# Turning the next unit's AT, G and K at other places of VectorE's order in a fused RWKV-7 and mixture kernel

## The chip, the core and the metric

The kernel runs on one core of a Trainium2 chip. The core has five engines with a queue of instructions each, and each runs its queue in order: TensorE (PE) multiplies matrices, VectorE (DVE) and GpSimd (POOL) work element by element, ScalarE (ACT) copies and activates, SyncE (SP) here only issues transfers. They wait for each other by semaphores. The metric is the time of one execution on the device, in microseconds; lower is better. Before the change the median of three runs is 1080.93 us (1078.75 to 1084.01).

## The reference

Two blocks follow each other. The first is a recurrence over 768 steps for 4 x 8 heads of width 40:

```python
y[:, :, t] = np.einsum('bhd,bhde->bhe', rt, state)
Sa = np.einsum('bhde,bhe->bhd', state, at)
state_decay = state * wt[:, :, None, :] - np.einsum('bhd,bhe->bhde', Sa, bt)
state = state_decay + np.einsum('bhd,bhe->bhde', vt, kt)
```

Its output, 3072 tokens of width 320, goes into four experts with 1024 hidden values each, whose outputs are added by normalized weights:

```python
for e in range(E):
    h = np.maximum(x @ w1[e], 0.0)
    out += p[:, e:e + 1] * (h @ w2[e])
```

All of it is fp32.

## The kernel before, in words

**Units.** The 768 steps are cut into 12 chunks of 64, and the 4 batches into 2 pairs. A chunk of one pair is a unit, `u` = 0 to 23. Inside a unit the recurrence is written as products of matrices: the decays are multiplied up along time (G), K and N (from b) are divided by them, A (AT) is multiplied by them, and a triangular system is solved for each head. The mixture for a chunk begins when both of its units are done, and its products are woven between those of the later units, so TensorE always has dense products beside the small ones.

**From unit 8 on** (`BY_CHANNEL`) the inputs of the next units come as raw tiles with heads and time side by side, and VectorE turns them: `turn_raw` (L324), a stream transpose. In one turn of the loop over `u`, work for several units is mixed, in the program's names:

- *G of unit u+3*: two turns out of rawW (L520), a scan (L566) that multiplies up along time, and the reciprocal `gp` (L582). `G0` is a memset of a column of it (L529).
- *AT*: one turn out of rawA, and the product with G (`AG`, L626). VT and RT are turned likewise.
- *N and K*: two turns each, out of rawB and rawK, then one product with `gp` (L640 and L645).
- *M, Z*: `blocks` (L722) are copied from F, the result of the products pfe; M is a transpose of them (L730) with its diagonal cleared (`M0`, L736); Z1 (L742) and Z2 (L746) take the first step of the substitution on VectorE. GpSimd then runs 48 short steps on Z (L760, L777), one behind the other, some 23 us. VectorE turns the result into Qc (L793) and QTc (L794), which the products pY, pQ and psat need. `merge` holds these.
- *RH* (L844): the sum behind the products prn. *Y, state* (L913 to L925): what is read from the products pdy. *ET, SX, VC*: masked copies (L499).

**The mixture on VectorE.** For an expert, the products of the hidden values with w2 are done by a scheme with seven products in place of eight. `add_h` (L1104) makes the five A sums of the hidden values: `a1`, `a7`, `a5`, `a2`, `a6`, named `sum_a0`, `sum_a1`, ... over the whole kernel, ten in each unit, so two groups of five. `down_1` multiplies p431, whose third term has `a1`; `down_2` multiplies p75 and p26, which use the other four. Their results are added to `osb` (L991, L993: "adds"). `down_1` of an expert follows on TensorE soon after its A sums were made, `down_2` much later.

**What sets the order.** A scheduler orders each engine's instructions by its own estimates and by what waits for what. On top, the kernel holds a list of stated orders for VectorE: pairs (one, then) without a semaphore, which only say which of two instructions comes first. `pin` and `keep` hold an instruction in program order instead. SP's queue is in program order: `later` is a list of transfers that are begun a few at a time between the pieces of the mixture (`mix` calls `begin_later`), or all at once with `begin_later(len(later))`. `load_piece` (L404) loads 640 KB of w1 in three transfers once TensorE has released the buffer.

The raw tiles and `gp` have one buffer each, `G` has three and `AT` two.

Of the kernel before, what the change touches and what calls it, by code (L numbers as in the profile page):

```python
# [33 lines left out]
def kernel(  # L34
# [46 lines left out]
    NJ = H // 2  # L81
    NF = F // P
    NU = NC * B // 2
# [6 lines left out]
    def noted(ins, name, n=None, i=None):  # L90
        if n is None:
            n = sum(k.startswith(name) for k in made)
        key = f"{name}{n}" if i is None else f"{name}{n}.{i}"
        made[key] = ins
        if key in names:
            stated_order.append(ins)
        return ins

    def keep(ins):

        if not any(ins is x for x in stated_order):
            tc.keep_in_program_order(ins)
# [109 lines left out]
    BY_CHANNEL = 8  # L212
# [32 lines left out]
    EARLY = 5  # L245
# [39 lines left out]
    def load_raw(q, names):  # L285


        moves = []
        for x in names:
            q.n["raw" + x] = t = raw[x]()  # L290
            heads = srcs[x].rearrange("b h t e -> (b h) t e")[q.b[0] * H:(q.b[1] + 1) * H, q.c * L:(q.c + 1) * L, :]
            heads = heads.rearrange("n (x two) e -> x n (two e)", two=2)
            for r in range(2):
                if x in "RV":

                    sets = ((slice(0, 8, 2), slice(r, 16, 4)), (slice(1, 8, 2), slice(3 - r, 16, 4)))
                else:
                    sets = ((slice(0, 8), slice(r, 16, 2)),)
                for n, hs in sets:
                    for y, w_ in enumerate((D + Q, 2 * D - Q)):  # L300
                        o = slice(64 * r + Q * y, 64 * r + Q * y + Q)
                        moves.append(lambda eng, out=t[o, n, 0:w_], in_=heads[:, hs, Q * y:Q * y + w_]: eng.dma_start(out=out, in_=in_))
        return moves
# [18 lines left out]
    def turn_raw(out, t):  # L322

        return nc.vector.transpose(  # L324
            out=out.rearrange("p n (x two) -> p n two x", two=2),
            in_=t.rearrange("p n (two e) -> p n two e", two=2)[:, :, :, 0:Q],
        )
# [173 lines left out]
    def within(q):  # L501

        n = q.n

        def pin(ins, also=False):
            if q.u <= PADDED or also:
                keep(ins)
# [3 lines left out]
        G = sb.tile([P, 2 * NJ, L + 1], FP32, name="G", tag="G", bufs=3)  # L511
        flat = G[:].rearrange("p c t -> p (c t)")
        if by_channel:
            q.G = Gv = G[:, :, 0:L]
            ahead = G[:, :, 1:L + 1].rearrange("p (j i) t -> p i j t", i=2)
        else:
            q.G = Gv = flat[:, 0:2 * NJ * L].rearrange("p (c t) -> p c t", t=L)
            ahead = flat[:, 1:2 * NJ * L + 1].rearrange("p (j i t) -> p i j t", i=2, t=L)
        for i in range(2):
            pin(noted(turn_raw(ahead[:, i], n["rawW"][:, NJ * i:NJ * i + NJ, :]), "G", q.u, i), EARLY + 2 < q.u < BY_CHANNEL + 3)  # L520
        if by_channel:
            q.gl = G[:, :, L:L + 1]
        else:
# [647 lines left out]
    todo, last, later, stores, here = [], [], [], [], [0]  # L1171

    def begin_later(n):
        for move in later[:n]:
            tc.keep_in_program_order(move(nc.sync))
        del later[:n]

    def mix(n):

        for piece in todo[:n]:  # L1180
            ready = stores[:]
            del stores[:]
            piece()
            for begin_store in ready:
                begin_store()
            begin_later(6 if here[0] % 4 == 0 and n > 1 else 3 if n > 1 else 6)
        del todo[:n]
# [5 lines left out]
    def run(gen, n=99):  # L1193
        if gen is None:
            return
        for _ in range(n):
            if next(gen, gen) is gen:
                break
# [3 lines left out]
    def begin_step(u):  # L1202
        q = units[u]
        if q.bp == 0:
            chunks_x[q.c] = sb.tile([P, 3, 2 * P], FP32, name="xT", tag="xT", bufs=2)
        q.xT = chunks_x[q.c][:, :, q.bp * P:(q.bp + 1) * P]
        return step(q, q.xT)
# [103 lines left out]
    for u in range(1, NU):  # L1311
        in_order[0] = True
        q = units[u]
        m = s_next = w = w_next = iter(())
        if u + 1 < NU:
            m, s_next = merge(units[u + 1]), begin_step(u + 1)
            w_next = ws[u + 1]
        if u + 2 < NU:
            w = ws[u + 2]

        def gap(n, pieces=None):
            here[0] = at = 4 * u + n
            run(sum_ops, sums_at.get(at, 0))
            mix((1 if at in sparse else 2) if pieces is None else pieces)

        early = u < EARLY
        if early:
            begin_later(len(later))
        ahead = u + 3 < NU and u >= EARLY
        if ahead and u < EARLY + 3:  # L1330
            go(load_raw(begin(u + 3), "W"))
        if early:
            lead()
        if u == 1:
            run(s, 1)
            run(w_next)
        else:
            run(w_next, 99 if early else 1)
            if u == EARLY:
                lead()  # L1340
            run(s, 1)
        gap(0)


        if early:
            run(s, 1)
        run(w, 1)
        if not early:
            run(w_next)
            run(s, 1)  # L1350
            if BY_CHANNEL <= u + 2 < NU:
                load_tokens(units[u + 2])
            run(s)

        if early:
            run(w, 1)
            gap(1, 2 if u + 1 == EARLY else None)
            run(s)
        if u == 1:
            mixture_of_unit(q)  # L1360
        elif q.bp:
            mixture_of_chunk(units[u - 1:u + 1], chunks_x[q.c])
        if not early:
            begin_later(len(later))
            run(w, 1)
            lead()
            todo[:2] = todo[1::-1]
            gap(1)
            run(m, 1)

        if u + 3 < NU:
            if u == 1:
                go_now(load_raw(begin(4), "WVRA"))
            else:
                go(load_raw(units[u + 3] if ahead else begin(u + 3), "A" if ahead else "WA"))
            load(units[u + 3], "V" if u + 3 >= BY_CHANNEL else "WBKV")
            if u > 1:
                later.extend(load_raw(units[u + 3], "VR"))
        run(w, 2)
        if BY_CHANNEL <= u + 2 < NU:  # L1380
            scale_tokens(units[u + 2])

        soon = u in (2, 3, 4)
        if soon:
            run(w, 1)
        if early:
            run(m, 1)
        else:
            run(m, 1)
            run(s_next, 1)  # L1390
            lead()
            run(m, 1)
            if u + 3 < NU:
                ws.append(within(units[u + 3]))
                run(ws[u + 3], 1)
        if soon:
            substitute(units[u + 2], nc.gpsimd)
        gap(2)

        if u == 1:  # L1400
            run(s_next, 1)
            run(m, 1)
        if not soon:
            run(w, 1)
        if not soon and u + 2 < NU:
            with sooner(not early):
                substitute(units[u + 2], nc.gpsimd)
        if not early:
            lead()
            run(s_next, 1)  # L1410
        if early:
            run(w, 1)
        if early:
            ws.append(within(units[u + 3]))
            run(ws[u + 3], 1)
            if u > 1:
                run(m, 1)
                run(s_next, 1)
            run(m)
            if u == 3:  # L1420
                begin_later(len(later))
            gap(3, 1)
            run(s_next, 1)
        else:
            begin_later(len(later))
            if BY_CHANNEL <= u + 3 < NU:
                if u + 3 == BY_CHANNEL:
                    pad_raw()
                later.extend(load_raw(units[u + 3], "BK"))
            gap(3)  # L1430
        if u >= EARLY + 2 and u + 4 < NU:
            later.extend(load_raw(begin(u + 4), "W"))
        s = s_next
# [5 lines left out]
    turned_ahead += [("QTc6", x) for x in ("VC7.0", "VC7.1", "sum_w15", "sum_w16")]  # L1439
    waits_of_scalar = [(f"SXc0.{n}", "RTc1.0") for n in range(4)]  # L1440
    ahead_of_merge = [(f"{x}{u}", f"Qc{u - 1}") for u in range(BY_CHANNEL, NU) for x in "KN"]
    ahead_of_merge += [(f"G{u}.{i}", f"Qc{u - 2}") for u in range(BY_CHANNEL + 3, NU) for i in range(2)]
    ahead_of_merge += [(f"VC{u}.{r}", f"1/gp{u + 1}") for u in range(BY_CHANNEL, NU - 1) for r in range(2)]
    ahead_of_merge += [(f"RH{u - 1}.{r}", f"1/gp{u + 1}") for u in range(BY_CHANNEL, NU - 1) for r in range(2)]
    ahead_of_merge += [(f"QTc{u - 1}", f"RH{u - 1}.{r}") for u in range(BY_CHANNEL, NU) for r in range(2)]
    ahead_of_merge += [(f"QTc{u - 1}", f"VC{u}.{r}") for u in range(BY_CHANNEL, NU) for r in range(2)]
    ahead_of_merge += [(f"1/gp{u + 2}", f"sum_a{10 * u - 45 + n}") for u in range(BY_CHANNEL, NU - 2) for n in range(5)]
    ahead_of_merge += [(f"M{u}", f"AT{u + 1}") for u in range(BY_CHANNEL, NU - 1)]
    in_second = [("Zr1.14", "out0"), ("out0", "Zm1.16")]
    for one, then in [*zip(names, names[1:]), *((f"out{n}", x) for n, x in moved), ("blocks0.3", "VCv1"), ("blocks0.3", "ETc0.0"), ("blocks1.3", "Zu1.0"), ("blocks1.3", "Zu1.3"), *turned_ahead, *in_second, *waits_of_scalar, *ahead_of_merge]:  # L1450
        tc.add_manual_dep(made[then].ins, made[one].ins.name, BEHIND, reason="stated order of VectorE")
# [30 lines left out]
```

## Time and profile before

| what | us |
|---|---|
| median of three runs | 1080.93 |
| the profiled execution | 1080.12 |
| its span on the core | 1078.4 |
| TensorE busy | 1052.9 |
| VectorE busy | 793.6 |
| GpSimd busy | 536.6 |
| ScalarE busy | 344.4 |

The span is what the engines record from first to last; the profiled execution's own time has 1.7 us more around it. A row of the timeline gives start, duration, engine, line of the code, operation, output and inputs with their shapes, and in brackets the idle time of the engine before it and what ended that. Rows of a group are merged with their number at the end (x4), and a duration is then that of all together. The duration of a row on VectorE overlaps the next by some 0.1 us, so the distance from row to row is shorter than the durations. In the waits a line names who waited for whom, the us in total, how often, and the longest.

### The profile page before, as it was taken

How to read it: one execution, taken by the hardware profiler on the slowest of the kernel's cores; microseconds unless marked ns; L12 is line 12 of the kernel's file. 1: busy time of each engine (PE TensorE's matmuls, PEld its weight loads, DVE VectorE, ACT ScalarE, POOL GpSimd, SP SyncE). 2: the span in 40 equal slices, each digit the busy share in tenths (PEclk: the TensorE clock that was granted, in tenths of full speed). 3: DMA queues.
4: the chain of work that ended last, by engine and by line, in shares of the span. 5: the costliest groups of instructions: out<-in, count | busy, mean ns of one | idle time of the engine just before them, and what ended most of it. 6: DMA issues, size and time to landing. Idle time of an engine off the chain costs nothing.

```text
span 1078.4 us, 38527 instructions
## 1 busy us (share of the span) xinstructions
PE 1052.9 (98%) x16022; PEld 945.3 (88%) x16022; DVE 793.6 (74%) x1565; ACT 344.4 (32%) x942; POOL 536.6 (50%) x1322
## 2 busy tenths in 40 slices
PE   8999999999999999999999999999999999999998
PEld 7888878888899889898998898898988999998887
DVE  7787679898778877777877878768777786634343
ACT  3433444423333323324233333242333333221110
POOL 6117677756375474563663744745636547520000
PEclk9999999999999999999999999999999999999999
DMA  6776644344443443543553563454444443121220
GB/s 115 189 206 140 143 101 117 81 101 107 109 102 96 112 111 71 138 104 78 117 124 67 106 143 58 108 125 90 98 121 95 98 108 91 55 72 51 75 86 13
DMA packets 275350, 111.05 MB, mean 103 GB/s; under 512 B 229816, under 2 KB 254952, under 8 KB 275176
## 3 DMA queue, kind: packets, MB, share of 16 engines
q1 hardware_dynamic: 271192, 107.75, 43.6%
q8 instruction: 126, 2.06, 0.8%
q10 hardware_dynamic: 3984, 0.84, 0.4%
q14 instruction: 48, 0.39, 0.1%
HBM read 100.65 MB, written 3.93 MB: 97 GB/s over the span
## 4 chain that ended last, share of the span: by engine, by line
PE 65%; POOL 14%; DVE 8%; issue 5%; DMA 4%; SPq 2%; ACT 2%; DVEq 0%; ACTq 0%; POOLq 0%
PE ph L110 27%; PE p L110 19%; POOL Z L777 8%; POOL Z L760 5%; PE po L110 3%; PE pdy L110 2%; PE prn L110 2%; PE psat L110 1%; PE pxr L110 1%; PE pfe L110 1%; PE pY L110 1%; PE pQ L110 1%; PE warm L110 1%; SPq L404 1%; DVE osb L993 1%
## 5 line engine op out<-in xcount | busy, mean ns | idle before, releaser
L777 POOL TENSOR_TENSOR Z<-Z 128x31 f32<-128x31 f32 (+7 forms) x704 | 261.3, 371 | 55.1
L1104 DVE TENSOR_TENSOR a<-hs 128x512 f32<-128x512 f32 x220 | 152.3, 710 | 102.6 <-ACT hs L978 102.6
L110 PE MATMUL ph<-xT,w1b 128*128 128x256 f32 (+3 forms) x1536 | 222.6, 374 | 0.5 <-issue 0.5
L110 PE MATMUL ph<-xT,w1a 128*128 128x256 f32 (+3 forms) x1536 | 221.0, 373 | 0.0
L978 ACT ACTIVATE hs<-ph 128x512 f32<-128x512 f32 (+1 forms) x208 | 117.0, 564 | 322.3 <-PE ph L110 320.5
L760 POOL TENSOR_TENSOR Z<-M,Z 128x62 f32<-128x62 f32 (+7 forms) x352 | 158.6, 450 | 112.0 <-DVE M L746 86.2
L110 PEld LDWEIGHTS ph<-xT,w1b 128*128 128x128 f32 (+1 forms) x1536 | 169.1, 161 | 27.6 <-issue 7.0
L110 PEld LDWEIGHTS ph<-xT,w1a 128*128 128x128 f32 (+1 forms) x1536 | 168.2, 161 | 28.2 <-issue 7.7
L993 DVE SCALAR_TENSOR_TENSOR osb<-p,gate,osb 128x320 f32<-128x320 f32 (+1 forms) x243 | 108.9, 482 | 82.2 <-PE p L110 77.5
L110 PE MATMUL p<-sums,a 128*128 128x160 f32 x1056 | 164.9, 299 | 0.0
L110 PEld LDWEIGHTS p<-sums,a 128*128 128x128 f32 x1056 | 152.8, 190 | 2.2
L727 POOL COPY below<-F 32x256 f32<-32x256 f32 x48 | 20.7, 432 | 174.0 <-ACT F L670 172.3
L110 PEld LDWEIGHTS p<-w,hs 128*128 128x128 f32 x704 | 98.6, 190 | 8.7 <-issue 7.4
L110 PE MATMUL p<-w,hs 128*128 128x160 f32 x704 | 104.9, 302 | 0.1
L110 PE MATMUL p<-w,a 128*128 128x160 f32 x704 | 102.8, 299 | 0.0
L110 PEld LDWEIGHTS p<-w,a 128*128 128x128 f32 x704 | 98.0, 190 | 0.0
L800 POOL COPY QT<-QTc 32x256 f32<-32x256 f32 x96 | 40.4, 421 | 68.5 <-DVE QTc L794 60.6
L898 ACT COPY RS<-pxr 64x256 f32<-64x256 f32 x88 | 32.3, 367 | 102.4 <-DMA rawB<-in_b_dram 47.7
L582 DVE RECIPROCAL gp<-G 128x512 f32<-128x512 f32 x16 | 53.5, 3343 | 0.1
L730 DVE STREAM_TRANSPOSE M<-blocks 128x1024 f32<-128x1024 f32 x24 | 47.4, 1975 | 3.3 <-ACT blocks L722 3.1
L708 ACT COPY EV<-pev 64x160 f32<-64x160 f32 x96 | 23.1, 286 | 83.8 <-PE pev L110 83.4
L670 ACT COPY F<-pfe 128x256 f32<-128x256 f32 x48 | 15.5, 376 | 80.1 <-PE pfe L110 79.0
(167 smaller groups left out, 1419.3 us busy)
## 6 DMA issues: line engine op xcount, KB each, us to landing
w1a<-in_moe_w_dram SPq DMA_DIRECT2D x37, 512.0 KB
w1b<-in_moe_w_dram SPq DMA_DIRECT2D x37, 512.0 KB
w<-in_moe_w_dram SPq DMA_DIRECT2D x4, 1280.0 KB
w1a<-in_moe_w_dram SPq DMA_DIRECT2D x74, 64.0 KB
w1b<-in_moe_w_dram SPq DMA_DIRECT2D x74, 64.0 KB
out_dram<-osb SPq DMA_DIRECT2D x45, 80.0 KB
rawW<-in_w_dram SPq DMA_DIRECT2D x48, 72.0 KB
natV<-in_v_dram SPq DMA_DIRECT2D x42, 80.0 KB
```

Of the source, the lines that this page charges most:

```text
L110: return stated(nc.tensor.matmul(**k))
L582: pin(noted(nc.vector.reciprocal(out=gp[:], in_=G[:, :, 1:L + 1]), "1/gp", q.u))
L708: nc.scalar.copy(out=of_slot(q.EV[half(p)], i ^ p)[:, :, 0:D], in_=pev[i][half(p)])
L727: tc.keep_in_program_order(nc.gpsimd.tensor_copy(out=q.below[quarter(i)], in_=q.F[quarter(i), :, 0:Q]))
L730: ins = nc.vector.transpose(out=M[:], in_=cols)
L760: ins = eng.tensor_tensor(out=Z[:, 1:3, 0:n, j + 1:Q], in0=M[:, j:j + 2, None, j + 1:Q].to_broadcast([P, 2, n, m]), in1=Z[:, here, 0:n, j: ...
L777: eng.tensor_tensor(out=z[:, 0], in0=z[:, 0], in1=z[:, x], op=ALU.add)
L800: ins = nc.gpsimd.tensor_copy(out=q.QT[quarter(i), :, quarter(i % 2)], in_=QTc[quarter(i)])
L898: nc.scalar.copy(out=RS[half(s), x ^ s::2], in_=prs[x][half(s)].rearrange("p (j i) t -> p j i t", i=2),)
L978: ins = nc.scalar.activation(out=h[:, i * HF // 2:(i + 1) * HF // 2, 0:n], in_=ph[i][:], func=ACTF.Relu,)
L993: ins = nc.vector.scalar_tensor_tensor(out=to, in0=p, scalar=sc, in1=to, op0=ALU.mult, op1=ALU.add)
L1104: ins = nc.vector.tensor_tensor(out=t[:], in0=x, in1=y, op=op)
```

## The change

Four edits, all for units from 8 on.

1. `AT{u+1}` was stated behind `M{u}`; it is now stated behind `Z2{u}`, the last step of M on VectorE.
2. G's turns were stated ahead of `Qc{u-2}` for later units. This is gone, and from unit 11 on G's turns are pinned in program order instead, as they were for units 8 to 10. In the built order they and the scan now come behind RH, with the reciprocal right behind them.
3. K and N of a unit were stated only ahead of `Qc`. They are now also stated ahead of five of the ten A sums of that unit, the second group.
4. On SP, raw B and K of unit u+3 are put into `later` before all of `later` is begun, not after it. So all eight transfers are begun in one go, ahead of the two pieces of w1 that follow; before, six came behind the first piece and two behind the second.
TensorE's, ScalarE's and GpSimd's instructions keep their order. On VectorE the scheduler places what is not stated: in the built kernel the group of five A sums that follows K comes ahead of Y in units with even K (and K9), and behind Y and the state in units with odd K from K11 on; in K8 the sums alternate with the adds, behind K.

```diff
@@ within
-            pin(noted(turn_raw(ahead[:, i], n["rawW"][:, NJ * i:NJ * i + NJ, :]), "G", q.u, i), EARLY + 2 < q.u < BY_CHANNEL + 3)
+            pin(noted(turn_raw(ahead[:, i], n["rawW"][:, NJ * i:NJ * i + NJ, :]), "G", q.u, i), q.u > EARLY + 2)
@@ the loop over u
-            begin_later(len(later))
             if BY_CHANNEL <= u + 3 < NU:
                 if u + 3 == BY_CHANNEL:
                     pad_raw()
                 later.extend(load_raw(units[u + 3], "BK"))
+            begin_later(len(later))
             gap(3)
@@ the stated order of VectorE
-    ahead_of_merge += [(f"G{u}.{i}", f"Qc{u - 2}") for u in range(BY_CHANNEL + 3, NU) for i in range(2)]
+    ahead_of_merge += [
+        (f"{x}{u}", f"sum_a{10 * (u - 1) - 50 + n}") for u in range(BY_CHANNEL, NU) for x in "KN" for n in range(5)
+    ]
@@
-    ahead_of_merge += [(f"M{u}", f"AT{u + 1}") for u in range(BY_CHANNEL, NU - 1)]
+    ahead_of_merge += [(f"Z2{u}", f"AT{u + 1}") for u in range(BY_CHANNEL, NU - 1)]
```

## The prediction

> **What bounds the kernel now.** I read the page's busy times, then the table of windows cut at one unit of work each, then TensorE's waits, then the timelines of TensorE, VectorE and GpSimd in two of these windows.
>
> ```profile
> PE 1052.9 (98%) x16022; PEld 945.3 (88%) x16022; DVE 793.6 (74%) x1565; ACT 344.4 (32%) x942; POOL 536.6 (50%) x1322
> ```
>
> TensorE is busy for 98% of the span, so an edit on VectorE can win at most TensorE's idle time, 25.5 us. Of that, 11.4 us lie in the windows up to 292 us and 3.6 us behind 986 us, which this change doesn't touch. In the stage that it touches, two neighbouring units are (columns: span of the window, then busy time of each engine):
>
> ```profile
> 617.56:659.86 42.30, 41.78 (x661) 38.06 (x661) 33.19 (x65) 13.86 (x38) 22.96 (x58) 1.00 0.54 121
> 659.86:703.10 43.24, 41.79 (x662) 38.19 (x661) 32.91 (x65) 13.86 (x38) 24.53 (x58) 1.00 0.40 86
> ```
>
> A unit is 41.8 us of TensorE work, whatever it lasts; the rest is idle. The waits of TensorE between 362 and 915 us have one cause:
>
> ```profile
> PE pY L110 <- DVE QTc L794: 9.6, 10, 1.5
> ```
>
> The pY products wait for QTc. On the timeline there are twelve such gaps from 359 to 870 us; 0.22, 1.07, 0.96, 0.51, 1.07, 1.14, 0.52, 1.45, 1.12, 1.24, 0.51, 0.18, in all 9.99 us (the last by its label behind pc, taken with them). Two more units have none (315 and 529 us), nor has the one at 911. I name a unit by the K that VectorE makes in it: these units are K9 to K23; K8, at 275 us, has a gap of 1.21 us as well, but its M, AT and scan keep their order.
>
> **What the change removes.** QTc is late for two reasons. In units with even K it is GpSimd: Z can only start behind M's last step Z2 (L746), and AT's turn and product, 0.68 and 0.69 us, stand ahead of that. In K16 Z2 ran at 589.34, behind VT too; Z ended at 613.34 and Qc began 613.37 after 0.51 us of waiting for it. In units with odd K Z ends as late (654.74 in K17), and VectorE adds to it: the scan stands between Qc and QTc:
>
> ```profile
> 654.03 0.76 DVE L324 STREAM_TRANSPOSE G<-rawW 128x256 f32<-128x256 f32 x2
> 654.78 0.63 DVE L793 STREAM_TRANSPOSE Qc<-Z 128x256 f32<-128x256 f32 x1
> 655.26 1.18 DVE L566 TENSOR_TENSOR_SCAN G<-G,first 128x520 f32<-128x520 f32 x1
> 656.35 0.42 DVE L794 STREAM_TRANSPOSE QTc<-Qc 128x256 f32<-128x256 f32 x1
> ```
>
> AT behind Z2: M ends 1.97 us behind its start at 584.90, Z1 and Z2 follow in 0.68 and 0.65 us, so Z2 ends near 588.3, not 589.99: Z starts 1.7 us sooner in K16, 1.2 us sooner in K17, where VT was not in front. AT is read by pfe in the next unit, 37 us later, and AG doesn't hold up anything: nothing on TensorE waits for them.
>
> G's turns and scan behind RH: VectorE then has 0.70 + 1.16 us more ahead of the reciprocal, which ran 616.81 to 620.15 and was followed by 1.73 us of waiting for hs. The first A sum would come at about 622.15, not 621.88, and a wait of 0.25 us at 623.42 (for p75) takes that up. F arrives at 626.94, so M keeps its place. Cost nothing; without that cover M would be 0.27 us later.
>
> Raw K in one go: on SP's queue the eight transfers of raw B and K, 0.49 us of issue each, go ahead of the two pieces of w1, between and around which they stood; raw W still follows the second. In even units the piece was waiting for TensorE to release it (rawR was issued by 584.2, w1b not before 588.78), so they fit in that wait and the 1.44 us in which KT waited for raw K at 605.36 is gone. In odd units w1b, issued at 633.23 without a wait, goes 3.9 us later, to 637.1 to 638.9. Its first reader is at 647.23. Raw K took 4.4 us from the end of its issue (600.93) to the turn that waited for it; nearest row for a piece, so w1b is there by about 644. Bounds: nothing, or 0.5 us a unit if a piece took twice as long; I take nothing. Raw W is issued 1 us sooner and its reader is later.
>
> With the scan gone and M sooner, would QTc be in time? In K16 the second p26 sum can be added at 602.47. From there VectorE has, by the spacing of rows of this unit: two adds 0.77, KT's turns and product 1.36, five A sums 3.15, the Y and state group with G's memset 2.66, four adds 1.57: Qc at 611.98, QTc ends 1.1 us later, pY could start at 613.23. TensorE is ready at 614.62 - 1.14 = 613.48. So a margin of 0.25 us, and none of the 1.14 is left; GpSimd, at 613.34 - 1.7, is done before. Gain: all 9.99 us. Bound on the other side: where A sums ran beside Z at 641.68 they took 0.74 us each, not 0.63, and five of them would cost 0.55 us, 0.3 more than the margin, in each of the eight units K9, K10, K12, ..., K22: 2.4 us. I take 0, from the spacing in K16 itself.
>
> **What the change adds.** All five A sums of the second half of a unit now stand behind K. The first of them, a1 (line 1099 names its operands), is the third term of p431, which TensorE runs soon after (p<-sums,a). Before, it was made some 8 us ahead. K17, TensorE:
>
> ```profile
> 647.32 0.25 PE L110 MATMUL pdy<-SX,n_tok 64*64 64x104 f32 x1
> 648.36 2.44 PE L110 MATMUL p<-w,hs 128*128 128x160 f32 x16
> 650.64 1.25 PE L110 MATMUL p<-sums,a 128*128 128x160 f32 x8
> 651.72 3.62 PE L110 MATMUL ph<-xT,w1b 128*128 128x256 f32 x16
> ```
>
> and VectorE in the same unit:
>
> ```profile
> 641.68 1.47 DVE L1104 TENSOR_TENSOR a<-hs 128x512 f32<-128x512 f32 x2 [3.23 <-ACT hs L978]
> 648.19 0.75 DVE L913 TENSOR_TENSOR Y<-pdy,RS 128x256 f32<-128x256 f32 x2
> 651.01 0.77 DVE L324 STREAM_TRANSPOSE KT<-rawK 128x256 f32<-128x256 f32 x2
> 652.39 0.68 DVE L645 TENSOR_TENSOR KT<-KT,gp 128x512 f32<-128x512 f32 x1
> ```
>
> The built kernel puts these in two ways. In the even units, and in K9, the order is N, the four adds of p75 and p26, K, five sums, then Y. There a1 ends at 602.47 + 0.77 + 1.36 + 0.65 = 605.25, and its reader is at 607.71: covered. In the seven units K11, K13, ..., K23 it is the four adds and N, then Y, the state, the turns and product of K, and only then the sums. Y waits for pdy, whose last product ends at 647.57. So a1 is behind TensorE: Y to G's memset 2.82 us (648.19 to 651.01), less 0.1 for a turn put into a gap of the state steps; KT's turns 0.70; K 0.61; a1 0.68; 4.7 us, ending at 652.3, and some 0.1 us for the release (pY came 0.15 us behind QTc's end). TensorE gets there at 650.64. It stands still for **1.75 us**, with p431's last term, ph and all that follows queued behind. Lower bound 1.45 (no release time, sums of the shortest spacing, 0.60); upper 2.1 (the steps at their busy means, not their spacing). Behind it pY has no wait: the five sums and four adds end at 656.3, QTc 1.1 later, while TensorE, 1.75 late, comes to pY at 658.2.
>
> **Sum.** 7 x 1.75 = 12.3 us added, 9.99 taken away: **+2.3 us**. The profiled execution took 1080.12 us (span 1078.4); the median, 1080.93, is 0.8 above it. On the median that gives 1083.2 us, 0.2% slower. Changes under about 0.5%, 5.4 us, can't be told from none here.
>
> **Rivals.**
>
> *Not late (faster).* If a1 were not behind TensorE in the odd units, all 9.99 us would show: 1071 us. It decides at 3.07 us, the time from pdy's end to p431's third term, against the 4.7 us of rows above; 1.6 us of VectorE work would have to vanish. For it: VectorE idles from 646.2 until pdy, so a different order could have used it. Against it: the built order, in which nothing but Y stands there. Chance 0.07.
>
> *GpSimd or VectorE still late in the even units (slower).* The margin is 0.25 us on VectorE, 0.6 on GpSimd. Steps of Z are drawn out by VectorE:
>
> ```profile
> 597.19 0.83 POOL L760 TENSOR_TENSOR Z<-M,Z 128x152 f32<-128x152 f32 x1
> 639.64 0.46 POOL L760 TENSOR_TENSOR Z<-M,Z 128x152 f32<-128x152 f32 x1
> ```
>
> In the first, N and the sums ran on VectorE; in the second it was idle. AG now runs beside Z, as the scan did and no longer does. Were Qc as late as now in the even units (0.74 us on the mean of K10 to K22, 5.19 us over seven), that much is not won: 1083.2 + 5.2 = 1088.4 us. For it: the thin margins. Against it: scan and AG about cancel (1.16 out, 0.61 in). Chance 0.18.
>
> [...]
>
> *Transfers.* w1b late in odd units: it decides 8.3 us behind the end of its issue (638.9 to 647.2). At 1 us for each of seven units 1090 us. Only the 4.4 us of raw K speak to it, and against. Chance 0.05.
>
> *The clock falls in the new gaps.* Each gap of 1.75 us could cost as much again, 12 us: 1095. The granted clock stayed at 1.00 in units with gaps of 1.45 us. Chance 0.02.
>
> [...]
>
> **How the numbers follow.** Forecast 0.68: 1081.1 to 1085.6 from the bounds of the wait alone (7 x 0.3 down, 7 x 0.35 up), 1088.0 with the 2.4 us of slower sums. The range leaves out the faster rival and the dearest: 1079 (the forecast's low end and some 2 us of the runs' own spread, 1078.75 to 1084.01) to 1089. Slower by over 0.5% (above 1086.3): the three slower rivals, 0.25, less the part of the second that stays below it, 0.04, and 0.03 for the forecast's upper end: 0.24. Faster by over 0.5% (below 1075.5): 0.07 and 0.01 for a gap partly gone. The rest, 0.68, is the same.
>
> **What would show it.** Right: TensorE's waits list p<-sums,a behind VectorE's A sums, about seven times, 1.5 to 2.1 us each, and the pY waits behind QTc are gone from 359 us on; units alternate between about 41.8 and 43.6 us; KT no longer waits for raw K; Z2 comes 1.2 to 1.7 us sooner behind blocks. Wrong: no wait at p431 (then 1071), or pY still waiting in even units (then above 1086), or ph waiting for w1b.

## The result

Twenty runs of each kernel: the median is 1079.94 us before and 1082.05 us after. One run of after took 6048.22 us and is left out of the ratio. The ratio is 1.0019 with a 95% interval of 1.0012 to 1.0026: 0.2% slower, inside the 0.5% that the prediction called the same, at 1082.05 where it said 1083.2. The profiled execution's span went from 1078.4 to 1080.3 us.

The page's busy times of after:

```profile
PE 1053.6 (98%) x16022; PEld 944.2 (87%) x16022; DVE 801.6 (74%) x1565; ACT 344.2 (32%) x942; POOL 527.6 (49%) x1322
```

TensorE stays the bound, and VectorE's and GpSimd's busy times barely say what happened. The waits of TensorE in after, 300 to 990 us (columns: us in total, times, the longest), do:

```profile
PE p L110 <- DVE a L1104: 9.7, 7, 1.4
PE pY L110 <- DVE QTc L794: 1.0, 3, 0.5
PE pY L110 <- PE pc L110: 0.7, 3, 0.2
PE pY L110 <- issue: 0.2, 1, 0.2
```

The 9.8 us for which pY waited for QTc are down to 1.0, and p431 (p<-sums,a) now waits 9.7 us for an A sum, seven times. Two neighbouring units of after in the table of windows (columns as before: span, then busy time of PE, PEld, DVE, ACT and POOL, the granted clock, the DMA share, GB/s):

```profile
657.70:699.20 41.50, 41.50 (x662) 37.93 (x660) 33.09 (x63) 13.81 (x39) 23.08 (x57) 1.00 0.43 90
699.20:742.90 43.70, 42.05 (x662) 38.02 (x660) 34.58 (x66) 13.88 (x39) 22.11 (x58) 1.00 0.49 115
```

Units now alternate: the first has TensorE busy throughout, the second is 2.2 us longer, and 1.65 us of it is idle time. K17, the unit just ahead of these, is the one whose order the prediction worked out. TensorE's timeline in it:

```profile
647.78 1.08 PE L110 MATMUL ph<-xT,w1b 64*64 64x256 f32 x14
648.79 2.44 PE L110 MATMUL p<-w,hs 128*128 128x160 f32 x16
652.62 1.35 PE L110 MATMUL p<-sums,a 128*128 128x160 f32 x8 [1.39 <-DVE a L1104]
```

and VectorE's:

```profile
648.04 0.76 DVE L913 TENSOR_TENSOR Y<-pdy,RS 128x256 f32<-128x256 f32 x2 [0.98 <-PE pdy L110]
...
650.22 0.43 DVE L324 STREAM_TRANSPOSE KT<-rawK 128x256 f32<-128x256 f32 x1
650.58 0.28 DVE L925 TENSOR_TENSOR state<-state,G 128x160 f32<-128x160 f32 x1
650.78 0.43 DVE L324 STREAM_TRANSPOSE KT<-rawK 128x256 f32<-128x256 f32 x1
651.17 0.07 DVE L529 MEMSET G<- 128x8 f32 x1
651.24 0.69 DVE L645 TENSOR_TENSOR KT<-KT,gp 128x512 f32<-128x512 f32 x1
651.85 3.16 DVE L1104 TENSOR_TENSOR a<-hs 128x512 f32<-128x512 f32 x5
```

Y, the state and K stand ahead of the first of five A sums. The row merges the five. The first of them alone ends at 652.56; TensorE was ready at 651.23 and started at 652.62.

The idle time of TensorE in the gaps followed here adds up to the difference: 9.71 us new at p431, 1.90 us left at pY on the timeline (a gap of 0.21 to 0.53 in each of seven even units; four of these seven stand in the waits under other names), 0.26 more at K8's pY (1.47 for 1.21), against 9.99 gone: +1.88 us. The spans differ by 1.9. So close a match is partly chance: by the page TensorE's whole idle time grew by 1.2 us and its busy time by 0.7.

So the total was right. What it was made of is another question: two sums of some 10 us that nearly cancel can both be wrong. The experiments take them apart.

### The profile page after: what moved, and what is told of

The parts are those of the page before. It is cut to its first block, busy times and chain, and to the rows that moved or that the text cites. A ratio compares the mean times of both kernels' runs of the same rounds, so it can differ in the third digit from the quotient of the medians.

```text
span 1080.3 us, 38526 instructions
## 1 busy us (share of the span) xinstructions
PE 1053.6 (98%) x16022; PEld 944.2 (87%) x16022; DVE 801.6 (74%) x1565; ACT 344.2 (32%) x942; POOL 527.6 (49%) x1322
## 4 chain that ended last, share of the span: by engine, by line
PE 76%; DVE 10%; POOL 8%; issue 2%; DMA 2%; ACT 1%; SPq 1%; DVEq 0%; POOLq 0%
PE ph L110 33%; PE p L110 25%; POOL Z L777 5%; POOL Z L760 3%; PE pdy L110 2%; DVE a L1104 2%; PE prn L110 2%; PE po L110 2%; PE pxr L110 2%; PE psat L110 2%; PE pfe L110 1%; PE warm L110 1%; PE pc L110 1%; PE pY L110 1%; PE pe L110 1%
## 5 line engine op out<-in xcount | busy, mean ns | idle before, releaser
L777 POOL TENSOR_TENSOR Z<-Z 128x31 f32<-128x31 f32 (+7 forms) x704 | 261.1, 371 | 55.1
L760 POOL TENSOR_TENSOR Z<-M,Z 128x62 f32<-128x62 f32 (+7 forms) x352 | 149.6, 425 | 95.3 <-DVE M L746 69.6
L1104 DVE TENSOR_TENSOR a<-hs 128x512 f32<-128x512 f32 x220 | 148.8, 710 | 41.2 <-ACT hs L978 41.2
```

Of the source, the lines that this page charges most:

```text
L760: ins = eng.tensor_tensor(out=Z[:, 1:3, 0:n, j + 1:Q], in0=M[:, j:j + 2, None, j + 1:Q].to_broadcast([P, 2, n, m]), in1=Z[:, here, 0:n, j: ...
L777: eng.tensor_tensor(out=z[:, 0], in0=z[:, 0], in1=z[:, x], op=ALU.add)
L1104: ins = nc.vector.tensor_tensor(out=t[:], in0=x, in1=y, op=op)
```

## The experiments

Each was compared with the kernel before, whose median was 1078.8 to 1079.5 us in these runs. "Edits" are the four of the change.

| run | kernel | median us | ratio to before, interval |
|---|---|---|---|
| e1 | edits 1, 2, 4 | 1067.07 | 0.988 (0.9856 to 0.9903) |
| e3 | all four, but the first A sum free of K | 1069.74 | 0.9903 (0.9881 to 0.9925) |
| e9 | all four, and the last of the five A sums ahead of Y | 1073.66 | 0.9948 (0.9936 to 0.9961) |
| e2 | edits 1, 2 | 1067.3 | 0.9875 (0.9849 to 0.9902) |
| e5 | edit 1 | 1075.75 | 0.9962 (0.9946 to 0.9979) |
| e6 | edit 2 | 1066.97 | 0.9886 (0.9871 to 0.9901) |
| e4 | edit 3 | 1112.98 | 1.0304 (1.0278 to 1.0329) |
| e7 | edits 1, 2, 3 | 1098.97 | 1.0181 (1.0159 to 1.0202) |
| e8 | e1, and K8's AT and VT behind Z2 | 1065.19 | 0.9871 (0.9858 to 0.9885) |
| e10 | edit 2, and K8's AT and VT behind Z2 | 1066.82 | 0.9887 (0.9872 to 0.9902) |

### e1: without the order of K, N and the sums

Theory: edit 3 alone makes the new wait, and without it the whole gain shows.

```diff
-    ahead_of_merge += [
-        (f"{x}{u}", f"sum_a{10 * (u - 1) - 50 + n}") for u in range(BY_CHANNEL, NU) for x in "KN" for n in range(5)
-    ]
```

> The changed kernel without the statement that K and N come ahead of five A sums; AT behind Z2, G behind RH and raw K in one go stay. Theory: the seven waits of p431 for a1 (7 x 1.39 us, and some 0.1 us each in which its first product is drawn out) go, and the short pY waits of the even units (0.2 to 0.5 us, 1.9 us in all) go with them, because the sums again fill VectorE's wait for p75 and p26: 1082.05 - 9.7 - 0.7 - 1.6 = 1070.0 us. Rival: K ahead of the sums is what brings QTc in time. Then pY waits for QTc again, 0.5 to 1.5 us in twelve units, and the time is about 1080 us, like before.

1067.07 us, 15 us less than after. TensorE doesn't stop from 362 to 915 us. The same window of before and then of e1:

```profile
362.00:915.00 553.00, 543.08 (x8583) 495.11 (x8582) 429.32 (x828) 180.28 (x495) 304.16 (x742) 1.00 0.47 104
```

```profile
362.00:915.00 553.00, 553.00 (x8725) 504.32 (x8724) 446.16 (x843) 184.49 (x504) 305.82 (x745) 1.00 0.46 104
```

The kernel gained some 3 us more than the idle time that went. The unit lengths say where that is: a unit of e1 takes 41.5 us from pc to pc, not the 41.8 of busy time that the prediction took as its floor. e6 below has the rows that explain it.

### e3: the first A sum free

The new wait is a matter of one sum. Here it alone is released from K; the other four stay behind.

```diff
-        (f"{x}{u}", ...) for u in range(BY_CHANNEL, NU) for x in "KN" for n in range(5)
+        (f"{x}{u}", ...) for u in range(BY_CHANNEL, NU) for x in "KN" for n in range(1, 5)
```

> The changed kernel, with K and N stated ahead of four of the five A sums; a1 alone is left free, and is built ahead of the adds. Theory: a1 alone holds TensorE. The seven p431 waits go; four sums and the adds still stand between K and Qc in the odd units, so QTc ends about 0.3 us late there: 1082.05 - 7 x 1.49 + 7 x 0.3 = 1073.7 us. Rival: the whole of VectorE's second half is late, not a1. Then what p431 no longer waits for comes back at pY, 1 us and more in the odd units, 1080 us.

1069.74 us. The wait at p431 is gone, and what is left of TensorE's waits from 362 to 915 us is

```profile
PE pY L110 <- PE pc L110: 1.4, 7, 0.2
```

seven gaps of 0.2 us in the odd units. So one sum made the whole of the new wait. The other four that remain behind K still fill VectorE up to Qc there: these gaps, and their lost overlap (below), are 3.0 us, and e3 is 2.7 above e1. It is 4 us under its expectation, which had let the 1.9 us of the even units stand; they are gone.

### e9: the five A sums ahead of Y

The same cause from the other side: K stays ahead of the sums, and the last of the five is stated ahead of the next Y. In the built order K and all five come ahead of Y.

```diff
+    ahead_of_merge += [(f"sum_a{10 * (u - 1) - 46}", f"Y{u - 2}.{i}") for u in range(BY_CHANNEL + 1, NU) for i in range(2)]
```

> The changed kernel with one statement more: the last of the five A sums ahead of Y, in every unit from K9 on. So the odd units get the order of the even ones: K, five sums, Y. Theory: the sums behind K cost little as long as Y and the state don't stand ahead of them. The seven p431 waits go; pY waits as shortly in the odd units as in the even ones, about 0.23 us of idle time and 0.23 us of lost overlap: 1082.05 - 7 x (1.39 + 0.23) + 7 x 0.46 = 1073.9 us. Rival: K's place ahead of the sums holds a1 too long anyway, p431 still waits, above 1078 us.

1073.66 us, with no wait at p431. TensorE's waits from 300 to 990 us:

```profile
PE pY L110 <- PE pc L110: 1.1, 5, 0.2
PE pY L110 <- DVE QTc L794: 0.5, 2, 0.3
```

It is Y behind pdy, and not K, that makes the sum late in the odd units: with K ahead of both, it is in time. What stands between this and e1 is pY just too late, in the even units by some 0.23 us of idle time, and in the odd ones by up to 0.15 us, too short for the list of waits (41.8 to 42.1 us a unit).

### e2, e5, e6: which edit removed the old waits

The prediction gave edit 1 the even units and edit 2 the odd ones. e2 has both, e5 the first, e6 the second.

```diff
@@ e2 and e5, edit 1
-    ahead_of_merge += [(f"M{u}", f"AT{u + 1}") for u in range(BY_CHANNEL, NU - 1)]
+    ahead_of_merge += [(f"Z2{u}", f"AT{u + 1}") for u in range(BY_CHANNEL, NU - 1)]
@@ e2 and e6, edit 2
-            pin(noted(turn_raw(...), "G", q.u, i), EARLY + 2 < q.u < BY_CHANNEL + 3)
+            pin(noted(turn_raw(...), "G", q.u, i), q.u > EARLY + 2)
-    ahead_of_merge += [(f"G{u}.{i}", f"Qc{u - 2}") for u in range(BY_CHANNEL + 3, NU) for i in range(2)]
```

> The kernel before with only two of the four edits: AT behind Z2, and G's turns and scan behind RH. Raw K in two parts, K and N not stated against the A sums. Theory: these two edits hold the whole gain, and raw K's waits are covered: pY doesn't wait from 359 us on, p431 doesn't either, 1070 to 1071 us. Rival: raw K begun in one go is needed. Then KT waits some 1.4 us for raw K in the even units and QTc is late there by 0.5 to 1 us, 1074 to 1078 us.

> The kernel before with only AT behind Z2. Theory: Z ends 1.2 to 1.7 us sooner, but the scan still stands ahead of QTc, so little is won. In the even units Qc can start when the adds behind the scan end, 612.86 and not 613.37 in K16: 0.5 us won of 1.14. In the odd units the scan between Qc and QTc keeps the 0.5 us of K17. Seven even units x 0.5 us less wait: 1079.5 - 3 = 1076.5 us. Rival: GpSimd's end of Z is what pY waits for everywhere, and the scan only fills a gap. Then all waits go, and the time is about 1068 us, like both edits together.

> The kernel before with only G's turns and scan behind RH. Theory: in the odd units QTc follows Qc at once and pY doesn't wait; in the even units Z still ends late (613.34 in K16) and the waits stay, 5.2 us of idle time over K10 to K22, with 0.23 us more each for the lost overlap (a unit without a wait lasts 41.54 us, one with a wait of 1.07 us 42.84 us): 1067.2 + 5.2 + 7 x 0.23 = 1074 us. Rival: the scan alone is the cause, 1068 us; or Z alone, then about 1079 us.

e2 took 1067.3 us and has no wait of TensorE from 300 to 990 us: edit 4 gives nothing beside edits 1 and 2. e5 took 1075.75, close to the expected 1076.5; its waits in that stretch:

```profile
PE pY L110 <- DVE QTc L794: 5.7, 9, 1.1
```

On the timeline the even units K10 to K22 now wait 1.1 us where they waited 5.2, the odd ones K11 to K21 4.6 where they waited 4.8. So edit 1 alone takes most of the even units' wait, and hardly any of the odd units'.

e6 fell out otherwise than the theory had it: 1066.97 us, all of the gain from edit 2 alone, which is what the rival expected. Its window of K17 (columns as above) is a unit without idle time, and its TensorE and VectorE rows at the end of K16 show QTc in time, with AT still ahead of Z2:

```profile
607.96:649.50 41.54, 41.54 (x662) 37.80 (x661) 33.63 (x64) 13.87 (x38) 22.81 (x58) 1.00 0.48 119
```

```profile
609.07 0.69 PE L110 MATMUL pc<-RT,VT 40*64 40x64 f32 x32
609.58 0.57 PE L110 MATMUL pY<-QTc,below 64*64 64x64 f32 x13
```

```profile
607.99 0.63 DVE L793 STREAM_TRANSPOSE Qc<-Z 128x256 f32<-128x256 f32 x1 [0.54 <-POOL Z L777]
608.65 0.45 DVE L794 STREAM_TRANSPOSE QTc<-Qc 128x256 f32<-128x256 f32 x1
```

Qc still waits for GpSimd here, but GpSimd is sooner. The steps of Z near its end, on GpSimd in K16, before and in e6:

```profile
609.79 1.66 POOL L777 TENSOR_TENSOR Z<-Z 128x35 f32<-128x35 f32 x2
```

```profile
605.14 0.94 POOL L777 TENSOR_TENSOR Z<-Z 128x35 f32<-128x35 f32 x2
```

Before, these two steps ran at 609.79 to 611.45, beside the scan on VectorE:

```profile
610.13 1.24 DVE L566 TENSOR_TENSOR_SCAN G<-G,first 128x520 f32<-128x520 f32 x1
```

In K17 of before, with no scan beside them, the same two steps took 0.62 us:

```profile
651.80 0.62 POOL L777 TENSOR_TENSOR Z<-Z 128x35 f32<-128x35 f32 x2
```

In e6 they took 0.94, with K's product beside them. In before the scan stands beside Z in all seven even units, K10 to K22, and in none of the odd ones from K11 on. The steps taken singly show what it does: in each of the seven, the first step of Z that begins with or after the scan lasts until 0.03 to 0.08 us behind the scan's end (611.45 against 611.38 in K16), 0.70 to 0.82 us longer than the same step in e6. Over the even units K10 to K22 the chain of Z, from its first step at L760 to its last at L777, lasted 23.00 us before, 22.20 in e6 and 23.46 in e5, where AG came to stand beside Z and the scan was still there. (Of the prediction's two rows of Z, the one at 597.19 had N's product alone beside it; the sums began at 598.76, behind it.)

How much of the lateness is this? In K16, from the step with 152 columns to the end, Z took 16.15 us before and 15.00 in e6: 1.15 less, 0.72 of it in the two steps above and 0.38 in the step with 152 columns, beside which other VectorE work ran. And Z2 came 0.51 us sooner (17.12 us behind the start of the last pY, for 17.63), since in before the scheduler had put VT's turn ahead of Z2 in this unit:

```profile
588.11 0.68 DVE L742 TENSOR_TENSOR Z<-M 128x512 f32<-128x512 f32 x1
588.71 0.71 DVE L324 STREAM_TRANSPOSE VT<-rawV 128x512 f32<-128x512 f32 x1
589.34 0.65 DVE L746 TENSOR_TENSOR M<-M,Z 128x512 f32<-128x512 f32 x1
```

and in e6 behind it, though no statement on VT had changed. Together Z ended 1.66 us sooner, where pY had waited 1.14. In K18, whose wait was the longest, 1.45 us, there was no VT ahead of Z2; Z was 1.23 us shorter in e6, and Z2 0.3 us sooner for reasons that I have not followed up. So in both the larger part is the shorter chain. Not all of the chain's change is the scan's: the one step that lasts until the scan's end is worth 0.70 to 0.82 us in each even unit, but the rest of VectorE's order moved too, and the chain as a whole was shorter by 0.2 (K14, K22) to 1.23 us (K18). No run holds VT and AT in place and moves the scan alone, so the shares rest on rows.

The two rows of TensorE fit the floor of 41.54 us. Without a wait pY starts at 609.58, while pc, which runs to 609.76, isn't done: 0.18 us of overlap. In before pY waited until long after pc's end. A unit with a 1.07 us wait lasted 42.84 us there, and 41.54 + 1.07 = 42.61: a wait at this place cost its idle time and some 0.23 us more. Twelve waits are 9.99 + 2.8 = 12.8 us, and 1079.94 - 12.8 = 1067.2, where e1, e2 and e6 lie.

### e4 and e7: K ahead of the sums without the early raw K

e4 is before with edit 3 alone; e7 is after with edit 4 undone.

```diff
@@ e4, against before
+    ahead_of_merge += [
+        (f"{x}{u}", f"sum_a{10 * (u - 1) - 50 + n}") for u in range(BY_CHANNEL, NU) for x in "KN" for n in range(5)
+    ]
@@ e7, against after
+            begin_later(len(later))
             if BY_CHANNEL <= u + 3 < NU:
                 ...
                 later.extend(load_raw(units[u + 3], "BK"))
-            begin_later(len(later))
```

> The kernel before with only the statement that K and N come ahead of five A sums. In the built order the sums then stand behind Y and the state in fourteen units, not seven. Theory: p431 waits for a1 in all fourteen, 1.4 to 1.8 us each, and because G's turns and scan still stand ahead of QTc, pY waits behind that, about 1.3 us more: 14 x 2.8 in place of 11.2 us, some 28 us slower, 1108 us (1095 to 1115). Rival: this order costs nothing by itself, 1080 us; or it costs only a1's wait and the pY waits go into it, 1080 + 14 x 1.5 - 11 = 1090 us.

> The changed kernel with raw K begun in two parts as before; AT, G and the order of K and N ahead of the sums stay. In the built order Y and the state then stand ahead of K and the sums in thirteen units, not seven. Theory: thirteen waits of p431 for a1, 1.4 to 1.7 us each and 0.23 us more of lost overlap, over 1067.2 us: 1088 to 1092 us. So raw K in one go matters only through the place that the scheduler gives K. Rival: the transfers matter by themselves or not at all, then 1082 us, or waits for rawK show ahead of TensorE's waits.

e4 took 1112.98 us, within its range; e7 1098.97, some 7 us above the upper end. The waits of TensorE from 250 to 990 us in e4:

```profile
PE p L110 <- DVE a L1104: 21.0, 14, 1.8
PE pY L110 <- DVE QTc L794: 13.5, 12, 2.2
```

and in e7:

```profile
PE p L110 <- DVE a L1104: 20.8, 13, 1.9
PE pY L110 <- DVE QTc L794: 4.1, 3, 1.4
```

With raw K late, the built order of e7 has Y ahead of K and the sums in 13 units in place of 7, so twice as many sums are late at p431. Edit 4 is no gain of its own (e1 against e2), but within the change it halves the price of edit 3: 1098.97 without it, 1082.05 with it. It does so by way of the scheduler's order, and by the wait for the transfer as well: in K16 of e7, which has the sums ahead of Y, KT waited 1.58 us for a transfer, and pY then 1.44 us for QTc.

e7's idle time in these waits is 24.9 us, in after 13.1 (9.71, 1.90, 1.47): 11.8 more, but the span is 16.6 longer. The rest is in the clock. TensorE and then the granted clock (next to the last three columns) in two windows of 3 us behind one gap of e7:

```profile
748.03 2.16 PE L110 MATMUL p<-sums,a 128*128 128x160 f32 x8 [1.88 <-DVE a L1104]
749.98 4.54 PE L110 MATMUL ph<-xT,w1a 128*128 128x256 f32 x16
```

```profile
748.00:751.00 3.00, 2.97 (x11) 2.79 (x12) 3.00 (x6) 0.00 (x0) 0.00 (x0) 0.57 0.16 37
751.00:754.00 3.00, 3.00 (x14) 2.56 (x13) 1.87 (x5) 0.60 (x1) 0.85 (x3) 0.86 0.18 46
```

The eight products took 2.16 us (1.35 behind the other gaps) and the sixteen behind them 4.54 (3.62): 1.7 us for one gap. Each fall of the clock is a stretch of 3.41 us at half of it; here is the first of e7's three (the clock is 0.50):

```profile
659.68:663.09 3.41, 3.41 (x12) 3.14 (x12) 3.40 (x8) 0.00 (x0) 0.00 (x0) 0.50 0.16 44
```

Three gaps of e7 did this, 5.1 us, which with the 11.8 us of idle time makes 16.9, near the 16.6. For e4 a part of the 34.8 us by which its span is longer stays without a name: 23.3 us more idle time in these waits and three falls of the clock at e7's 1.7 leave some 6 us.

### e8 and e10: K8 as well

K8's pY gap, 1.21 us before and 1.47 after, belongs to a unit in which none of the edits moves M. e8 is e1 with one pair of statements more, e10 is e6's kernel with the same.

```diff
+    ahead_of_merge += [(f"Z2{BY_CHANNEL - 1}", f"{x}{BY_CHANNEL}") for x in ("AT", "VT")]
```

> The changed kernel without the order of K and N ahead of the sums, and with AT and VT of unit 8 behind Z2 of unit 7 as well, the one unit whose M, AT and VT kept their order. Theory: Z of that unit starts 1.2 us sooner, so pY's wait of 1.47 us at 275 us falls to 0.3 us: 1067.1 - 1.2 = 1065.9 us. Rival: that Z waits for something else, then 1067.1 us.

> The kernel before with G's turns and scan behind RH, and AT and VT of unit 8 behind Z2 of unit 7; nothing else of the change. Theory: AT behind Z2 in the later units, raw K in one go and the order of K add nothing to G's place, so this is as fast as the fastest kernel so far: 1065.2 us. Rival: AT's place, or raw K, is worth a part of a us here: 1066 to 1067 us.

K8's gap in e8:

```profile
274.48 0.59 PE L110 MATMUL pY<-QTc,below 64*64 64x64 f32 x13 [0.23 <-DVE QTc L794]
```

1065.19 and 1066.82 us. With AT and VT behind Z2 the gap is down to 0.23 us in e8 and gone in e10, so they were the cause; which of the two, or both, no run tells. The time of e10 is the one that its rival named, but the intervals of the two overlap each other's and e6's, so these runs don't rank them; all three are 1.1 to 1.3% faster than before.

## Why the prediction was right, and where it was wrong

**The wait at p431: right in place, count and cause; too long by 0.36 us.** Seven odd units, K11 to K23, the first A sum, Y and the state and K ahead of it: all seen, and e1, e3 and e9 show the cause. The term "7 x 1.75" was 7 x 1.39 = 9.71. Of the difference, VectorE's stretch from Y's start to the end of the sum was 4.52 us, not 4.71 (0.19), TensorE needed 3.19 us from Y's start to the third term, not some 3.07 (0.12), and the release took 0.06 us, not 0.1. Even the lower bound, 1.45, was above it: it varied the release and the sum alone, which are worth 0.18 us and not the 0.30 that it took off, and it took Y's group with the spacing that it has in another order.

**"Gain: all 9.99 us": nearly right, with the wrong remainder.** 1.90 us stayed at pY in the even units, against a margin of 0.25 us that was said to leave none. The prediction named the weak point, five A sums beside Z: in K16 they came 0.70 us apart (606.21 to 609.69 for five), not 0.63, which is 0.33 us in all, K's turns and product took 1.57 for 1.36, and from the second p26 sum to K's first turn it was 1.14 us for 0.77, with 0.16 of waiting for a transfer in it. That is the second rival, at a third of its price and with VectorE late, not GpSimd: in K16 Z ended at 611.95, and Qc began at 613.77 behind the adds, without a wait. The rows of after, VectorE and GpSimd:

```profile
606.21 3.55 DVE L1104 TENSOR_TENSOR a<-hs 128x512 f32<-128x512 f32 x5
613.77 0.63 DVE L793 STREAM_TRANSPOSE Qc<-Z 128x256 f32<-128x256 f32 x1
```

```profile
611.43 0.52 POOL L777 TENSOR_TENSOR Z<-Z 128x8 f32<-128x8 f32 x2
```

K8's gap, called untouched, grew by 0.26 us. Two terms were wrong, by 2.6 us downward at p431 (12.3 to 9.71) and by 2.2 upward here: they nearly cancel, and +2.3 became +1.9. That the sum was right to 0.1% is luck in good part.

**Edit 1 for the even units: half wrong.** "In units with even K it is GpSimd" held: in before Qc waited for it there. And AT ahead of Z2, the reason that it gave, is one reason: in after Z2 of K16 came 16.04 us behind the start of the last pY, for 17.63, and e5, which moves AT alone, takes 4.1 of the even units' 5.2 us. But it is not what had to go: e6 leaves AT there and removes all the waits. The step that failed is the one that counted the scan as a delay between Qc and QTc in the odd units only, and set it against AG in the even ones with "scan and AG about cancel". Without the scan beside it (e6) Z's chain was shorter by 0.8 us on the mean, with AG beside it as well as the scan (e5) longer by 0.46, and the first was enough with the place that the scheduler then gave to VT. Edit 1 by itself gives 0.4% (e5), as the odd units keep their waits; beside edit 2 it gives nothing that these runs can tell (e2 against e6). The forecast's number doesn't hang on this, as both edits were in it: the 9.99 us were gone by either way.

**"A unit is 41.8 us": 0.26 us too long.** In the rows of e6, where neither pc nor pY waits, their busy times overlap by 0.18 us. It didn't show in the forecast, since twelve waits went and fourteen came or stayed; it made the expectation for e1 3 us too high. The idle time behind 986 us, given as 3.6 us, is 3.95; nothing hangs on it.

**Raw K in one go, taken at nothing: right as a term, wrong as a reading.** KT's wait for raw K, 1.44 us in K16, is gone, and no transfer of w1 was late at ph, so the third rival did not occur. But e7 shows that edit 4 is worth 17 us inside this change, mostly because the place of K in the built order hangs on it.

**The clock.** It stayed at 1.00 behind all gaps of after that this change made or left, the longest 1.47 us, so this rival fell there. It was nearer than the prediction had it: e7 had three falls, behind gaps of 1.88 to 1.91 us, and one of them took 1.7 us more, about as much again as its gap (the last section has them all).

## What to carry to other kernels

Where one engine is 98% busy, the sum to make is idle time at its waits, edit by edit, and each edit is worth a run of its own: here edit 2 alone wins 1.1%, and edit 3 gave it all back, most of it through one of five sums that came 1.4 us behind its reader. A stated order "x ahead of all of a group" is best checked against the earliest reader in the group. When a chain on GpSimd is late, look at what VectorE runs beside it before moving its start: here it took 23.00 us in the even units of before, with a scan beside it, and 22.20 in e6, without.

## What the runs showed of the hardware

- **The granted clock fell behind six gaps of 1.85 to 2.21 us.** Between 250 and 990 us TensorE has sixteen gaps above 1.2 us in e4 and sixteen in e7. Behind every gap up to 1.84 us the clock of the next 3 us was 1.00; behind all five from 1.88 to 2.21 us it was 0.52 to 0.69; of two gaps of 1.85 us one was followed by 1.00 and one by 0.71. By these 32 gaps, what parts the two is where they lie. Each of the six falls lasted 3.41 us at 0.50, and the falls of one run start whole multiples of 3.413 us apart (659.68, 748.42 and 837.17 in e7; 633.05, 762.76 and 813.96 in e4). When the time is cut into stretches of 3.413 us in step with the falls, the gap ahead of each fall lies within the one stretch that ends where the fall starts, with 1.85 to 2.21 us of it idle. The other 26 gaps put at most 1.79 us into one stretch, and the 1.85 us that cost nothing lay across two (0.25 and 1.60).
- **A wait between small products cost more than its idle time**, some 0.23 us here: a unit of before with a wait of 1.07 us lasted 42.84 us, one of e6 without a wait 41.54.
- **A GpSimd step that began beside a scan on VectorE ended with the scan**, 0.03 to 0.08 us behind its end, in all seven even units of before. Two steps of 35 elements each took 1.66 us there in K16, 0.62 in K17, where no scan ran. The chain that they belong to was 0.8 us shorter on the mean where a scan of some 1.2 us had been moved away from it.
